# Loading the first strided values once instead of twice, in a fused attention and feed-forward kernel with a newly searched order

## The chip, the cores and the metric

The kernel runs on one core of one Trainium2 chip. The metric is device time in microseconds (us) for the whole program. The profiled execution is one run recorded by the hardware profiler; its span is the time from the core's first to its last instruction. Engines are named as in the profile: PE (matmul), PEld (its weight load), DVE, ACT, POOL and SP. SPq and ACTq are the sequencers of SP and ACT, from which transfers are issued.

## The reference

```python
def _attn_ref(q, k, v):                      # 8 batches, 8 heads, 576 positions, 64 channels
    scores = scale * np.matmul(q, k.transpose(0, 1, 3, 2))
    mask_local = (rel >= 0) & (rel < 32)                       # heads 0 to 3
    mask_strided = (rel >= 0) & (pos[None, :] % 32 == pos[:, None] % 32)   # heads 4 to 7
    scores = np.where(masks[None], scores, -1e9)
    attn = exp(scores - max) / (sum + 1e-9)
    return np.matmul(attn, v)

def _moe_ref(x, w_in, w_out, g_ln):          # x: 4608 tokens x 512
    h = x @ w_in                             # 512 x 1024
    sm = softmax(h)
    solu = h * sm
    ln = (solu - mean) / sqrt(var + 1e-6) * g_ln
    return ln @ w_out                        # 1024 x 512
```

The weights `w_in` and `w_out` arrive as 64-bit floating point numbers and are decoded on the chip.

## The kernel before

Each batch has two kinds of attention heads. Local heads look back over 32 positions, strided heads look at positions of the same residue modulo 32. The work of a batch is cut into five units: units 0 and 1 are the strided heads, units 2 to 4 the local ones. Unit numbers run on, so that unit 5 is the first of batch 1. A unit is a chain: `qk` (PE, lines 419 and 424), the row maximum, subtraction, sum and reciprocal (DVE, lines 430 to 438), the exponential (ACT, 432), the scaling (POOL, 441), an fp16 upper part (ACT, 446) and lower part (POOL 448 or DVE 450), a transpose of the probabilities through a DMA from `p` to `pt` (SP, 452), `pv` (PE, 473) into `x_ps`, and the fp16 upper and lower parts of the result, `xhi` (ACT, 489) and `xlo` (DVE, 490). The banks of `x_ps` that `pv` writes must have been read by the steps 489 and 490 of an earlier unit.

The feed-forward part takes 36 tiles of 128 tokens: `g1` (PE, 531 to 533, two halves of 12 matmuls) makes h from `xhi`, `xlo` and the two fp16 parts of `w_in`; DVE and ACT make the normalised rows (538 to 559), a DMA transposes them (570), and `g2` (PE, 574 to 576) multiplies with the two parts of `w_out`.

Weights come in four loads of 1 MB each for `w_in` and four for `w_out`, into the four rooms `room0`, `room1`, `eu0` and `eu1`. Each load is decoded by two ACT steps (599 and 600) and one DVE step (601). From the decoded `w_in` a power-of-two scale is made (`gram` on PE, line 295, then `pow2_scale`), and with it the two fp16 parts: the upper one on ACT (617), the lower one on DVE (619) or, for half of the weights, on PE (`rest`, 627 and 628) followed by an ACT copy (631). `w_out` has its own `gram` over the four decoded pieces, then `split_o` (653 and 654).

The values of batch 0's strided heads have a path of their own. They are loaded twice from HBM in the same layout into the buffer `vtwo`: `t0` into partitions 0 to 63 (from ACT's queue), `t1` into partitions 64 to 127 (from SP's queue). ACT then writes the fp16 upper part into all 128 partitions of `vd` (374, two instructions), and DVE the lower part into partitions 0 to 63 (375). The upper half of the partitions holds the upper part a second time, so that one pass of `pv` multiplies both parts of the probabilities. The scale for these values is made from a `gram` over all of `vtwo` and `vrl`. Later batches load 128 partitions once and spread the parts with copies inside SBUF (394).

All steps are recorded by `plan.add` with the data that they read and write, and are then emitted in the order of the table `ORDER`, which lists step numbers. Each engine's and each queue's own order follows from that table. A DMA for which an instruction waits stands in its issuer's order, and what stands behind it on that queue waits with it.

Of the kernel before, what the change touches and what calls it, by code (L numbers as in the profile page):

```python
# [13 lines left out]
ALU = mybir.AluOpType  # L14
# [3 lines left out]
B, H, S, D = 8, 8, 576, 64  # L18
# [3 lines left out]
P = 128  # L22
# [140 lines left out]
def attn_solu_kernel(ctx: ExitStack, tc: tile.TileContext, qloc, qstr, kloc, kstr, vloc, vstr, w_in, w_out, g, masks, out):  # L163
    nc = tc.nc
# [70 lines left out]
    def load(name, dst, src, w):  # L235
        e, q = ("act", nc.scalar) if name in ACTQ else ("sp", nc.sync)
        add(e, lambda: q.dma_start(dst, src), w=w)
# [515 lines left out]
```

## Time and profile before

| | |
|---|---|
| median of 3 runs | 506.12 us (504.93 to 506.67) |
| the profiled execution's own time | 507.28 us |
| its span, first to last instruction | 505.6 us |
| mean granted TensorE clock | 0.993 |
| PE busy | 473.5 us (94%) |
| DVE busy | 354.2 us (70%) |
| ACT busy | 294.0 us (58%) |
| POOL busy | 151.0 us (30%) |
| moved by DMA | 96.51 MB, mean 191 GB/s |
| read from HBM | 40.03 MB |

The rows of a timeline have the start in us, the length in us, the engine and line, the operation, the tile written and the tile read, the number of instructions, and in brackets the idle time of that engine just before them with what ended it. A row that covers several instructions starts with the first of them. The rows of transfers give the packets, bytes and rate of a stretch, or the issues of a kind with their size and the median time from issue to landing. Rows of stretches give, by engine, the busy time in us and the number of instructions, then the granted clock as a share of full speed, the busy share of the 16 DMA engines (which can exceed 1 where packets overlap) and GB/s. What lies between the end of the span and the execution's own time is 1.68 us.

### The profile page before, as it was taken

The page shows a single profiled execution, that of the slowest core. Times are in us where ns is not written, and L with a number is a line of the kernel's source. Part 1 is how long each engine was busy: PE and PEld are TensorE (multiplying, and loading weights), DVE is VectorE, ACT ScalarE, POOL GpSimd, SP SyncE. Part 2 cuts the span into 40 slices and gives each one's busy share as a digit, 9 for nine tenths or more (in the row PEclk, how much of TensorE's full clock was granted, in tenths as well). Part 3 has the DMA queues.
Part 4 walks back from the last instruction along what each step waited for, and adds up shares of the span by engine and source line. Part 5 has one row for each costly group of instructions (what it writes and reads, how often), then busy time and mean ns, then how long its engine had stood idle before and what let it go on. Part 6 is the DMA issues. An engine that isn't in the chain of part 4 may idle for free.

```text
span 505.6 us, 11821 instructions
## 1 busy us (share of the span) xinstructions
PE 473.5 (94%) x4858; PEld 246.7 (49%) x4858; DVE 354.2 (70%) x679; ACT 294.0 (58%) x414; POOL 151.0 (30%) x258
## 2 busy tenths in 40 slices
PE   2557999999999999999999999999999999999997
PEld 1444554455544554454544554455444555444443
DVE  2688798785873797589865986487954989645530
ACT  1698877853746557546646446653756466344631
POOL 3234153444150133305330153301430053312330
PEclk9998899999999999999999999999999999999999
DMA  8999999688977879966998999977977797652361
GB/s 256 397 327 269 306 196 176 184 200 186 191 152 205 215 174 171 274 158 150 172 250 179 201 206 217 232 181 163 219 164 203 165 191 129 116 106 62 88 141 64
DMA packets 168294, 96.51 MB, mean 191 GB/s; under 512 B 138032, under 2 KB 154800, under 8 KB 167728
## 3 DMA queue, kind: packets, MB, share of 16 engines
q1 hardware_dynamic: 162624, 84.77, 78.6%
q10 hardware_dynamic: 5616, 10.98, 6.5%
q8 instruction: 38, 0.62, 0.5%
q14 instruction: 16, 0.13, 0.1%
HBM read 40.03 MB, written 9.44 MB: 98 GB/s over the span
## 4 chain that ended last, share of the span: by engine, by line
PE 81%; DMA 9%; DVE 6%; issue 2%; ACT 1%; SPq 1%; POOL 0%; DVEq 0%; ACTq 0%
PE h_ps L531 12%; PE o_ps L574 11%; PE h_ps L532 11%; PE h_ps L533 11%; PE o_ps L575 11%; PE o_ps L576 11%; PE x_ps L473 5%; PE s_ps L424 5%; DMA vrl<-vloc 3%; DMA eu<-w_out 2%; PE s_ps L419 1%; DMA pt<-p 1%; DMA vtwo<-vstr 1%; DMA ct<-c 1%; PE s_ps L576 1%
## 5 line engine op out<-in xcount | busy, mean ns | idle before, releaser
L441 POOL TENSOR_TENSOR t<-t,m 128x576 f32<-128x576 f32 (+2 forms) x40 | 51.4, 1287 | 238.7 <-DVE m L438 180.0
L531 PE MATMUL h_ps<-w,xhi 128*128 128x512 f16 x280 | 106.6, 381 | 0.0
L532 PE MATMUL h_ps<-w,xhi 128*128 128x512 f16 x280 | 106.1, 379 | 0.0
L533 PE MATMUL h_ps<-w,xlo 128*128 128x512 f16 x280 | 106.1, 379 | 0.0
L574 PE MATMUL o_ps<-obuf,ct 128*128 128x512 f16 x272 | 103.4, 380 | 0.6 <-DMA ct<-c 0.5
L576 PE MATMUL o_ps<-obuf,ct 128*128 128x512 f16 x272 | 103.1, 379 | 0.0
L575 PE MATMUL o_ps<-obuf,ct 128*128 128x512 f16 x272 | 103.1, 379 | 0.0
L538 DVE TENSOR_REDUCE st<-h_ps 128x1 f32<-128x1024 f32 x35 | 42.7, 1220 | 39.5 <-PE h_ps L533 38.8
L549 ACT ACTIVATE eu<-h_ps,st,vsc 128x1024 f32<-128x1024 f32 x31 | 37.3, 1204 | 36.4 <-DVE st L539 31.1
L556 ACT ACTIVATE c<-eu,st 128x1024 f16<-128x1024 f32 x36 | 41.2, 1145 | 24.3 <-DVE st L555 22.8
L557 DVE SCALAR_TENSOR_TENSOR c<-eu,st,c 128x1024 f16<-128x1024 f32 x36 | 46.9, 1304 | 10.7 <-ACT c L556 10.6
L552 DVE SCALAR_TENSOR_TENSOR eu<-h_ps,st,eu 128x1024 f32<-128x1024 f32 x35 | 44.8, 1279 | 8.4 <-ACT eu L549 7.2
L424 PE MATMUL s_ps<-k,q 64*54 64x54 f32 (+1 forms) x1280 | 41.6, 272 | 5.4 <-DMA k<-kloc 3.7
L432 ACT ACTIVATE t<-t 128x576 f32<-128x576 f32 (+2 forms) x40 | 27.4, 686 | 31.9 <-DVE t L431 30.7
L533 PEld LDWEIGHTS <-xlo 128*128 128x128 f16 x288 | 28.2, 98 | 34.2 <-issue 0.3
L576 PEld LDWEIGHTS <-ct 128*128 128x128 f16 x288 | 28.2, 98 | 34.0
L531 PEld LDWEIGHTS <-xhi 128*128 128x128 f16 x288 | 28.2, 98 | 33.8 <-ACT w L631 0.7
L559 ACT ACTIVATE junk<-eu,st 128x1024 bf16<-128x1024 f32 x36 | 41.1, 1141 | 6.0 <-DVE st L555 3.7
L574 PEld LDWEIGHTS <-ct 128*128 128x128 f16 x288 | 28.1, 98 | 33.1 <-DMA ct<-c 1.0
L532 PEld LDWEIGHTS <-xhi 128*128 128x128 f16 x288 | 28.2, 98 | 31.4 <-issue 0.3
L575 PEld LDWEIGHTS <-ct 128*128 128x128 f16 x288 | 28.2, 98 | 30.5
L424 PEld LDWEIGHTS s_ps<-k,q 64*54 64x54 f32 (+1 forms) x1280 | 39.6, 199 | 6.2 <-issue 6.2
(148 smaller groups left out, 682.0 us busy)
## 6 DMA issues: line engine op xcount, KB each, us to landing
out<-ob ACTq DMA_DIRECT2D x36, 256.0 KB, 3.3
vtwo<-vstr SPq DMA_DIRECT2D x8, 768.0 KB, 6.8
vd<-vtwo SPq DMA_DIRECT2D x14, 384.0 KB, 6.9
vrl<-vloc SPq DMA_DIRECT2D x8, 640.0 KB, 6.2
k<-kstr SPq DMA_DIRECT2D x8, 594.0 KB, 5.2
q<-qloc SPq DMA_DIRECT2D x8, 576.0 KB, 5.8
k<-kloc SPq DMA_DIRECT2D x8, 576.0 KB, 6.6
q<-qstr SPq DMA_DIRECT2D x7, 594.0 KB, 5.6
```

The lines of the kernel that those rows point to most:

```text
L424: nc.tensor.matmul(s_ps[row : row + nq, pair, i * nk : (i + 1) * nk], q_raw[half][hs, q0 : q0 + (nq - 1) * nqb + 1 : nqb], k_raw[half][hs, ...
L441: add("pool", lambda: nc.gpsimd.tensor_tensor(tv, tv, sm.unsqueeze(2).broadcast_to([P, nx, nk]), op=ALU.mult), r=TM, w=[T])
L531: nc.tensor.matmul(hv[:, i], xhi[:, cc, tok], whi[:, cc, cols], start=(cc == 0), stop=False)
L532: nc.tensor.matmul(hv[:, i], xhi[:, cc, tok], wlo[:, cc, cols], start=False, stop=False)
L533: nc.tensor.matmul(hv[:, i], xlo[:, cc, tok], whi[:, cc, cols], start=False, stop=(cc == 3))
L538: add("dve", lambda: nc.vector.tensor_reduce(low, hv, axis=AX.XY, op=ALU.max, negate=True), r=HH, w=[(ST, "low")])
L552: add("dve", lambda: nc.vector.scalar_tensor_tensor(uv, hv, ia, ev, op0=ALU.mult, op1=ALU.mult, accum_out=us), r=[*HH, E, (ST, "ia")], w=[ ...
L556: add("act", lambda: nc.scalar.activation(c[:, 0], u, AF.Identity, bias=mean, scale=1.0), r=[U, (ST, "mean")], w=[(C, 0)])
L557: add("dve", lambda: nc.vector.scalar_tensor_tensor(c[:, 1], u, mean, c[:, 0], op0=ALU.add, op1=ALU.subtract), r=[U, (ST, "mean"), (C, 0)] ...
L574: nc.tensor.matmul(o, ct[:, cc, :], ohi[:, cc, :], start=(cc == 0), stop=False)
L575: nc.tensor.matmul(o, ct[:, cc, :], olo[:, cc, :], start=False, stop=False)
L576: nc.tensor.matmul(o, ct[:, 8 + cc, :], ohi[:, cc, :], start=False, stop=(cc == 7))
```

## The change

The load `t1` is dropped. The `gram` for the scale reads partitions 0 to 63 of `vtwo`, the two ACT steps write 64 partitions, and for each of them a DMA inside SBUF copies the upper part to partitions 64 to 127 of `vd`; `pv` of batch 0's strided units waits for these copies too. Two step numbers are added and one dropped, and the table `ORDER` is another one throughout.

```diff
 ORDER = [
-    11, 6, 10, 9, 14, 0, 13, 31, 15, 5, 18, 16, 2, 19, 7, 12, 4, 3, 69, 70, 71, 82, 72, 73, 58, 1, 74, 32, 83, 75, 8, 84, 17, 23, 76, 27, 126, 59, 143, 85,
+    11, 6, 10, 9, 30, 4, 13, 14, 18, 7, 17, 0, 22, 15, 2, 12, 3, 8, 1, 16, 5, 26, 70, 71, 72, 83, 73, 31, 74, 57, 262, 75, 32, 84, 76, 85, 33, 86, 58, 77, 19,
...
     def load_v(b, a):
         if b == 0 and a:
-            for i in range(2):
-                load(f"t{i}", vtwo[i * D : i * D + D].rearrange("p (y f) -> p y f", y=2), vstr[b].rearrange("(y p) f -> p y f", y=2),
-                     [("vr2", 1)] if i else [("vr", 1), ("v", 1, 0), ("v", 1, 1)])
+            load("t0", vtwo[0:D].rearrange("p (y f) -> p y f", y=2), vstr[b].rearrange("(y p) f -> p y f", y=2), [("vr", 1), ("v", 1, 0), ("v", 1, 1)])
             return
...
-            gram(vm[:, 0:1], [(vtwo, [("vr", 1), ("vr2", 1)]), (vr_sb[0], [("vr", 0)])], ("vm", 0, 0), (o_ps[:, 0:P], "o"), (junk[:, 0:P], "junk"))
+            gram(vm[:, 0:1], [(vtwo[0:D], [("vr", 1)]), (vr_sb[0], [("vr", 0)])], ("vm", 0, 0), (o_ps[:, 0:P], "o"), (junk[:, 0:P], "junk"))
...
-            R = [("vr", 1), ("vr2", 1), ("vsc", 0), ("v", 1, 0), ("v", 1, 1)]
+            R = [("vr", 1), ("vsc", 0), ("v", 1, 0), ("v", 1, 1)]
             for y in range(2):
-                hi, lo = vd_sb[:, 0, :, y], vd_sb[0:D, 1, :, y]
-                add("act", lambda y=y, hi=hi: nc.scalar.mul(hi, raw[:, :, y], sc[:, 1:2]), r=R, w=[("v2", 1, y)])
-                add("dve", ... stt(lo, raw[0:D, :, y], sc[0:D, 1:2], hi[0:D], ...), r=[*R, ("v2", 1, y)], w=[("v2", 1, 2 + y)])
+                hi, lo = vd_sb[0:D, 0, :, y], vd_sb[0:D, 1, :, y]
+                add("act", lambda y=y, hi=hi: nc.scalar.mul(hi, raw[0:D, :, y], sc[0:D, 1:2]), r=R, w=[("v2", 1, y)])
+                add("sp", lambda y=y, hi=hi: nc.sync.dma_start(vd_sb[D:P, 0, :, y], hi), r=[("v2", 1, y)], w=[("v2", 1, 4 + y)])
+                add("dve", ... stt(lo, raw[0:D, :, y], sc[0:D, 1:2], hi, ...), r=[*R, ("v2", 1, y)], w=[("v2", 1, 2 + y)])
...
-        VV = [("v2", half, i) for i in range(4 if half else 3)] + ...
+        VV = [("v2", half, i) for i in range(6 if half and b == 0 else 4 if half else 3)] + ...
```

The order of each queue moves with the table. In the rows below a name's last number is that of the buffer in the program, and the numbers before it are the kernel's own (`room1`, `eu0`). The first place is SP's queue from the start of the program. Before:

```order
L237 DMA k10_66<-kstr 128x1188
L237 DMA vtwo0_72<-vstr 64x2x1536
L237 DMA room1_68<-w_in 128x2048
L237 DMA vrl0_70<-vloc 128x1280
L237 DMA g0_124<-g 128x8
L237 DMA q00_63<-qloc 128x1152
L237 DMA eu0_103<-w_in 128x2048
L237 DMA k00_65<-kloc 128x1152
L237 DMA eu1_104<-w_in 128x2048
L237 DMA room0_67<-w_in 128x2048
```

After, the same stretch and on to the first transpose:

```order
L237 DMA room1_68<-w_in 128x2048
L237 DMA vrl0_70<-vloc 128x1280
L237 DMA eu0_103<-w_in 128x2048
L237 DMA g0_124<-g 128x8
L237 DMA eu1_104<-w_in 128x2048
L237 DMA q00_63<-qloc 128x1152
L237 DMA k00_65<-kloc 128x1152
L237 DMA room0_67<-w_in 128x2048
L237 DMA k10_66<-kstr 128x1188
L237 DMA vrl0_70<-vloc 128x1280
L373 DMA vd0_73<-vd0_73 64x6x256
L237 DMA vtwo0_72<-vstr 128x1536
```

The `t1` load (`64x2x1536`) is gone, the loads of `eu0` and `eu1` have moved ahead of `q00` and `k00`, batch 1's `k10` is loaded before its values, and the two copies `vd<-vd` stand around batch 1's `vtwo` load (the second right behind the last row shown).

The second place is SP's queue around the four loads of `w_out`. Before:

```order
L237 DMA room0_67<-w_out 128x2x1024
L452 DMA_TRANSPOSE pt1_100<-p1_97 128x10x128
L237 DMA room1_68<-w_out 128x2x1024
L394 DMA ve0_74<-vl0_71 64x2560
L452 DMA_TRANSPOSE pt0_99<-p2_98 128x12x128
L237 DMA eu1_104<-w_out 128x2x1024
L237 DMA eu0_103<-w_out 128x2x1024
```

After:

```order
L237 DMA room0_67<-w_out 128x2x1024
L451 DMA_TRANSPOSE pt1_100<-p1_97 128x10x128
L393 DMA ve0_74<-vl0_71 32x2x1024
L237 DMA eu0_103<-w_out 128x2x1024
L393 DMA ve0_74<-vl0_71 64x2560
L451 DMA_TRANSPOSE pt0_99<-p2_98 128x12x128
L237 DMA room1_68<-w_out 128x2x1024
L237 DMA eu1_104<-w_out 128x2x1024
```

Two of the four loads stand ahead of unit 2's transpose (`pt0<-p2`) in both; the other two follow it, as `eu1`, `eu0` before and as `room1`, `eu1` now.

The third place is ACT's queue where these loads are decoded and where the last pieces of `w_in`'s lower part are copied (`w16<-h_ps`), with unit 1's and unit 2's `xhi`. Before:

```order
L599 ACTIVATE obuf0_121<-room1_68 128x1024
L446 CAST p0_96<-t3_90 128x6x96
L489 CAST xhi0_101<-x_ps_129 128x2x18x15
L599 ACTIVATE obuf0_121<-room0_67 128x1024
L600 ACTIVATE room1_68<-room1_68,consts0_116 128x1024
L631 CAST w160_120<-h_ps_128 128x512
L489 CAST xhi0_101<-x_ps_129 128x2x192
L631 CAST w160_120<-h_ps_128 128x512
L600 ACTIVATE room0_67<-room0_67,consts0_116 128x1024
L631 CAST w160_120<-h_ps_128 128x512
L599 ACTIVATE obuf0_121<-eu0_103 128x1024
```

After:

```order
L598 ACTIVATE obuf0_121<-room0_67 128x1024
L488 CAST xhi0_101<-x_ps_129 128x2x18x15
L445 CAST p0_96<-t3_90 128x6x96
L630 CAST w160_120<-h_ps_128 128x512
L431 ACTIVATE t1_88<-t1_88 128x648
L599 ACTIVATE room0_67<-room0_67,consts0_116 128x1024
L598 ACTIVATE obuf0_121<-eu0_103 128x1024
L488 CAST xhi0_101<-x_ps_129 128x2x192
L630 CAST w160_120<-h_ps_128 128x512 x2
L599 ACTIVATE eu0_103<-eu0_103,consts0_116 128x1024
L630 CAST w160_120<-h_ps_128 128x512
L598 ACTIVATE obuf0_121<-room1_68 128x1024
```

Before, the first decode of `w_out` that ACT meets is that of the second load (`room1`), and unit 1's `xhi` stands behind it. Now it is that of the first load (`room0`), and the decodes follow in the order of the loads.

More of the change, by code (lines that the diff above doesn't have):

```diff
@@ L370, in v_split @@
             raw = vtwo.rearrange("p (y c f) -> p c y f", y=2, c=6)
-            R = [("vr", 1), ("vr2", 1), ("vsc", 0), ("v", 1, 0), ("v", 1, 1)]
+            R = [("vr", 1), ("vsc", 0), ("v", 1, 0), ("v", 1, 1)]
             for y in range(2):
-                hi, lo = vd_sb[:, 0, :, y], vd_sb[0:D, 1, :, y]
-                add("act", lambda y=y, hi=hi: nc.scalar.mul(hi, raw[:, :, y], sc[:, 1:2]), r=R, w=[("v2", 1, y)])
-                add("dve", lambda y=y, hi=hi, lo=lo: nc.vector.scalar_tensor_tensor(lo, raw[0:D, :, y], sc[0:D, 1:2], hi[0:D], op0=ALU.mult, op1=ALU.subtract), r=[*R, ("v2", 1, y)], w=[("v2", 1, 2 + y)])
+                hi, lo = vd_sb[0:D, 0, :, y], vd_sb[0:D, 1, :, y]
+                add("act", lambda y=y, hi=hi: nc.scalar.mul(hi, raw[0:D, :, y], sc[0:D, 1:2]), r=R, w=[("v2", 1, y)])
+                add("sp", lambda y=y, hi=hi: nc.sync.dma_start(vd_sb[D:P, 0, :, y], hi), r=[("v2", 1, y)], w=[("v2", 1, 4 + y)])
+                add("dve", lambda y=y, hi=hi, lo=lo: nc.vector.scalar_tensor_tensor(lo, raw[0:D, :, y], sc[0:D, 1:2], hi, op0=ALU.mult, op1=ALU.subtract), r=[*R, ("v2", 1, y)], w=[("v2", 1, 2 + y)])
             return
@@ L474, in pv @@
                                              start=(a == 0), stop=(a == len(passes) - 1))
-        VV = [("v2", half, i) for i in range(4 if half else 3)] + (["vz"] if half else []) + ([("v", 0, 0), ("v", 0, 1)] if half == 0 else [])
+        VV = [("v2", half, i) for i in range(6 if half and b == 0 else 4 if half else 3)] + (["vz"] if half else []) + ([("v", 0, 0), ("v", 0, 1)] if half == 0 else [])
         add("pe", pv, r=[PT, *VV], w=X)
```

94 rows, old and new, of the table ORDER are left out of this document.

## The prediction

> **What bounds the kernel now.** I read the span by stages first. After the stretch and its length, the columns are PE, PEld, DVE, ACT and POOL busy, the granted clock, the DMA share and GB/s.
>
> ```profile
> 0.00:50.00 50.00, 25.71 (x444) 18.99 (x444) 32.97 (x67) 31.96 (x36) 16.49 (x37) 0.97 1.03 311
> 50.00:70.00 20.00, 18.21 (x184) 9.80 (x184) 16.57 (x34) 15.23 (x21) 6.94 (x5) 0.91 1.16 264
> 70.00:480.00 410.00, 407.69 (x4131) 208.23 (x4131) 300.11 (x572) 240.62 (x350) 123.10 (x207) 1.00 0.85 178
> 480.00:505.60 25.60, 21.88 (x102) 9.72 (x100) 4.54 (x8) 6.21 (x9) 4.43 (x11) 0.99 0.43 105
> ```
>
> From 70 to 480 us PE idles 410.00 − 407.69 = 2.3 us: PE is the bound there. The edited loads lie in the first 50 us, where PE idles 24.3 us and the DMA engines are full (share 1.03). The change can win only by letting PE's dense stretch begin earlier. So I read PE's timeline from its last long gap on.
>
> ```profile
> 46.79 1.12 PE L627 MATMUL h_ps<-c,wdiag 128*128 128x512 f32 x2
> 47.76 0.38 PE L628 MATMUL h_ps<-w,minus 128*128 128x512 f16 x1
> 50.61 0.28 PE L473 MATMUL x_ps<-pt,ve 96*64 96x64 f16 x6 [2.48 <-DVE xlo L490]
> 51.55 2.08 PE L627 MATMUL h_ps<-c,wdiag 128*128 128x512 f32 x2
> 53.85 0.61 PE L531 MATMUL h_ps<-w,xhi 128*128 128x512 f16 x1
> 59.04 0.38 PE L533 MATMUL h_ps<-w,xlo 128*128 128x512 f16 x1
> 63.83 0.63 PE L295 MATMUL o_ps<-obuf 128*128 128x128 bf16 x8 [0.57 <-DVE obuf L601]
> 64.30 0.38 PE L531 MATMUL h_ps<-w,xhi 128*128 128x512 f16 x1
> 67.35 0.16 PE L315 MATMUL o_ps<-o_sc,ones 128*128 128x1 bf16 x1 [0.30 <-DVE o_sc L645]
> ```
>
> Unit 2's `pv` starts at 50.61 after 2.48 us idle, tile 0's `g1` runs from 53.85 to about 59.3, tile 1's starts at 64.30. Two waits hold this stretch back. Both lead to ACT and the decode of `w_out`.
>
> ```profile
> 47.60 1.14 ACT L599 ACTIVATE obuf<-room 128x1024 f32<-128x1024 f32 x1 [1.30 <-DMA room<-w_out]
> 49.21 0.60 ACT L489 CAST xhi<-x_ps 128x540 f16<-128x540 f32 x1
> 52.31 0.47 ACT L489 CAST xhi<-x_ps 128x384 f16<-128x384 f32 x1
> 52.69 0.58 ACT L631 CAST w<-h_ps 128x512 f16<-128x512 f32 x1
> 56.83 1.14 ACT L599 ACTIVATE obuf<-eu 128x1024 f32<-128x1024 f32 x1 [1.96 <-DMA eu<-w_out]
> ```
> ```profile
> 49.84 0.72 DVE L490 TENSOR_TENSOR xlo<-x_ps,xhi 128x540 f16<-128x540 f32 x1 [1.11 <-ACT xhi L489]
> 60.88 1.22 DVE L538 TENSOR_REDUCE st<-h_ps 128x1 f32<-128x1024 f32 x1
> 62.56 1.21 DVE L601 SCALAR_TENSOR_TENSOR obuf<-obuf,eu 128x1024 int32<-128x1024 int32 x1
> ```
>
> ACT waits until 47.60 for the second `w_out` load, unit 1's `xhi` (49.21) and `xlo` (49.84) follow late, and PE's gap ends with that `xlo`. The fourth load reaches ACT at 56.83; its last decode step on DVE ends at 63.77, and PE's last `gram` matmuls wait for it.
>
> **The change part by part.** *Loads and copies.* The price of the DMA's time comes from three stretches (packets, MB, rate) and the issue row of the later batches' like copies.
>
> ```profile
> DMA packets 425, 2.37 MB, mean 279 GB/s; under 512 B 45, under 2 KB 45, under 8 KB 364
> DMA packets 728, 4.39 MB, mean 419 GB/s; under 512 B 83, under 2 KB 89, under 8 KB 343
> DMA packets 703, 0.35 MB, mean 176 GB/s; under 512 B 16, under 2 KB 703, under 8 KB 703
> vd<-vtwo SPq DMA_DIRECT2D x2, 192.0 KB, 5.2
> ```
>
> The first is 5 to 13.5 us, with `t0` and `t1` in it; the second is 18 to 28.5, of big loads; the third is 62 to 64, only 512-byte copies into `vd`. `t1` is 64 x 3072 x 4 B = 0.786 MB: 2.8 us at 279 GB/s. If it cost no more than any other load it is 1.9 us at 419; if the two half-partition loads caused the whole shortfall of that stretch (2.37 MB would take 5.65 us at 419, so 2.85 us) it is 1.9 + 2.85 = 4.7. The two copies move 0.393 MB: 2.2 us at 176 GB/s, 0.9 at 419, and at most 2.6 if each held the engines for half of the 5.2 us that its kind takes to land. I take the middle values, since these rows hold the same shapes: −2.8 + 2.2 = −0.6 us of DMA time, with ends −3.8 and +0.7.
>
> The Trainium skill, page "SBUF — State Buffer", section "Can I just issue two DMAs to hit both halves?", states that two transfers to partitions 0 and 64 serialise, with 6% gained; its "Door 1" section gives 64 partitions about half the ports. An estimate from its 196 GB/s for 64 partitions would make `t1` 4.0 us, the copies 2.0, and the sum −2.0 instead of −0.6. The trace agrees in direction (279 against 419 GB/s), and the high end above covers it.
>
> *Other work of this part.* ACT's two steps on 64 partitions cost what they did on 128:
>
> ```profile
> 23.36 3.53 DVE L375 SCALAR_TENSOR_TENSOR vd<-vtwo,vsc,vd 64x1536 f16<-64x1536 f32 x2
> 46.94 1.79 DVE L380 SCALAR_TENSOR_TENSOR vtwo<-vtwo,vsc 128x1536 f16<-128x1536 f32 x1
> 21.34 3.03 ACT L374 ACTIVATE vd<-vtwo,vsc 128x1536 f16<-128x1536 f32 x2
> 23.51 0.33 SPq L237 DMA_DIRECT2D vrl<-vloc  x1
> 26.92 0.34 SPq L237 DMA_DIRECT2D vtwo<-vstr  x1
> 36.15 0.94 PE L473 MATMUL x_ps<-pt,vd 118*64 118x54 f16 x48
> ```
>
> The shorter `gram` also stays as long. The copies wait for ACT, whose steps end at 24.4; SP before it waits anyway until 23.51 and 26.92 to issue batch 1's values, so no queue is held longer. Issued by 27.3, at 5.2 us the copies land near 32.5, ahead of unit 0's `pv` at 36.15: 3.6 us of cover, so I cost them at nothing on PE. If they landed over 3.6 us late, PE would still have its other idle time there.
>
> *The queue orders.* Unit 2's transpose and the four loads:
>
> ```profile
> 32.55 0.39 SPq L237 DMA_DIRECT2D room<-w_out  x1
> 39.04 0.57 SPq L237 DMA_DIRECT2D room<-w_out  x1
> 40.38 4.87 SPq L452 DMA_TRANSPOSE pt<-p  x1
> pt<-p SPq DMA_TRANSPOSE x1, 9.8
> 45.97 10.84 DMA eu<-w_out
> ```
>
> The fourth row is the landing time of that transpose: 40.38 + 9.8 = 50.2. In the new order ACT's first decode uses the first load, issued 6.5 us before the second, so 1.30 us of waiting disappear and unit 1's `xlo` no longer ends PE's gap. What is late next is the transpose, at 50.2 − 0.6 = 49.6. Unit 2's `pv` moves from 50.61 to 49.6: −1.0 us.
>
> *Up to the first `g1`.* Between `pv` and `g1` stand 2 + 1 `rest` matmuls. They take 53.85 − 51.55 = 2.30 us here and 48.14 − 46.79 = 1.35 at 46.79. The clock rows say why.
>
> ```profile
> 46.00:48.00 2.00, 2.00 (x38) 1.13 (x34) 1.97 (x4) 0.70 (x2) 0.83 (x1) 1.00 1.72 106
> 51.00:52.00 1.00, 1.00 (x25) 0.94 (x21) 0.90 (x3) 1.00 (x2) 0.00 (x0) 0.50 0.98 393
> ```
>
> The granted clock is 0.50 after the 2.48 us gap and 1.00 before it. With PE's work still ending near 48.1 the gap shrinks to 1.5 us or less, and I assume that the clock stays up. That gives 0.95 us, of which ACT takes 0.25 back: `pv` ends at 50.5, then `xhi` (0.47) and two copies (0.58 each) bring `g1` to 52.2 rather than 51.9. So `g1` starts 1.7 us earlier; with the clock halved, 1.0.
>
> The Trainium skill, page "TensorE: Matmul & The Clock Gate", section "What's actually happening", lets the clock halve after an idle window of about 3.4 us. Here 2.48 us was enough, so the measurement decides; by the page the shorter gap would keep the full clock.
>
> *From tile 0 to tile 1.* With 0.2 us more gained where tile 0's first matmuls ran at half clock, it ends at 59.3 − 1.9 = 57.4. The last load lands at 45.97 + 10.84 = 56.8, minus 0.6 = 56.2; its two ACT steps (about 1.1 each) end at 58.4. On DVE the row reduction after tile 0 (1.22), small steps (0.46, the space before 62.56) and the last decode (1.21) end near 60.3. The DVE steps for the scale follow, and their PE step now stands ahead of tile 1's `g1`. Here that step runs at 67.35, 3.6 us after the decode's end at 63.77, with steps of other units and tiles in between; in the new order fewer stand there, and I take 2.0, which is an estimate (at 3.6 tile 1 would start at 64.0). So tile 1 starts at 62.4 instead of 64.30 (−1.9). The wait of 0.30 at 67.35 is gone too. Sum: **−2.2 us**.
>
> *The rest.* The profiled execution took 507.28 us, 1.16 above the median of 506.12. 507.28 − 2.2 = 505.1; put on the median, **503.9 us**. In the middle the order is new throughout, but PE's waits from 68 to 480 are small, so little can be won there. The two longest (total, times, longest):
>
> ```profile
> PE x_ps L473 <- DMA pt<-p: 0.8, 1, 0.8
> PE o_ps L574 <- DMA ct<-c: 0.5, 1, 0.5
> ```
>
> I count it as 0, with ±2.3 us, its whole idle time, as bounds. The tail after 480 has nothing of the change in it.
>
> **The rivals.** *The gain is eaten.* The copies take 2.6 us and the dropped load saves only 1.9, so the transpose lands at 50.9, 0.3 us after the start of today's `pv`; the gap stays long enough for the clock to halve, and tile 1 waits as today. That gives −0.1 to −0.5, about 505.8. For it: the DMA engines are full until 66 us and a DVE chain of 3.6 us instead of 2.0 would by itself hold tile 1 until 64.0. Against it: ACT's waits of 1.30 and 1.96 go by the order alone.
>
> *A larger relief.* The half-partition load cost 4.0 us, so the transpose and the last load land about 2 us earlier rather than 0.6. The start of tile 1 then hangs on DVE alone, and tile 0 ends 0.9 us sooner: −3.1, 503.0.
>
> *Slower: a transpose comes late in the new order.* In the old order one unit, 24, had 21.7 us of PE's work between its `qk` and its `pv` (added up over the order with the rows' durations) and waited 0.8 us for `pt`, the first row above. In the new order unit 33 has 19.7, before 33.8. If its chain takes unit 24's 22.5 us, PE idles 2.8 us, and a gap of that length halves the clock as at 50.61, where it cost 0.95 + 0.2 us and can cost twice that in a stretch of nothing but PE's work: 4.5 in all, 506.12 − 2.2 + 4.5 = 508.4. It decides when the stall costs over 3.7 us. Against it: other units ran with 15.6 (unit 14) and 18.2 (unit 29) and never waited.
>
> **How the numbers follow.** Some 0.3%, 1.5 us, is about what a measurement of this kernel can tell from no change, so under 504.6 is faster and over 507.6 slower. Forecast 0.43, its own range 502.6 to 505.0, five sixths of it faster; gain eaten 0.27; larger relief 0.14; late transpose 0.16, of which 0.02 stays under 507.6. Faster: 0.36 + 0.14 = 0.50. Same: 0.07 + 0.27 + 0.02 = 0.36. Slower: 0.14. The range runs from 501.6 (larger relief, and half of the middle's idle time won) to 507.0 (gain eaten, and a small new wait), and leaves out most of the late transpose.
>
> **What would show it.** Right: ACT's first decode of `w_out` starts before 46 without a wait; PE's gap before unit 2's `pv` under 1.6 us, granted clock 1.00 at 51; first `g1` near 52.2, tile 1's near 62.4; the copies into `vd` landed before 33. Wrong: a gap ended by the transpose after 50.5, a clock of 0.50 again, or any wait of PE over 1 us between 70 and 480.

## The result: 1.1% slower

The changed kernel takes 511.41 us (median of 4 runs, 511.25 to 512.29) against 506.39 us for the kernel before on the same measurement; the ratio is 1.0108, with a 95% interval from 1.0084 to 1.0132. Forecast was 503.9. The profiled execution has a span of 509.5 us (before: 505.6). Its stages, in the columns of the prediction (PE, PEld, DVE, ACT, POOL busy, clock, DMA share, GB/s; the last stretch runs past the end of the span):

```profile
0.00:50.00 50.00, 24.67 (x444) 19.32 (x445) 34.44 (x69) 33.65 (x37) 20.14 (x37) 0.97 1.03 305
50.00:70.00 20.00, 18.13 (x208) 10.26 (x208) 17.31 (x36) 14.94 (x21) 6.59 (x6) 0.91 1.17 256
70.00:480.00 410.00, 404.73 (x4100) 206.30 (x4093) 297.70 (x568) 237.51 (x345) 123.76 (x209) 1.00 0.85 178
480.00:520.00 40.00, 25.87 (x120) 11.56 (x118) 6.17 (x10) 8.36 (x13) 2.85 (x8) 0.99 0.34 73
```

PE's total busy time is the same in both (473.4 and 473.5 us), so the 3.9 us of span come out as idle time: 1.1 us more in the first 70 us (27.2 against 26.1), 3.0 us more from 70 to 480 (5.27 against 2.31), and nothing in the tail. Matmuls at half clock take longer and count as busy, so these figures alone don't say where the delay arises. Where PE's dense stretch begins, the new kernel reads so:

```profile
9.78 1.50 PE L423 MATMUL s_ps<-k,q 64*54 64x54 f32 x48 [3.02 <-DMA q<-qstr]
50.11 0.37 PE L472 MATMUL x_ps<-pt,ve 96*64 96x64 f16 x6 [2.31 <-DVE vsc L361]
51.21 2.08 PE L626 MATMUL h_ps<-c,wdiag 128*128 128x512 f32 x2
53.47 0.38 PE L530 MATMUL h_ps<-w,xhi 128*128 128x512 f16 x1
61.98 0.63 PE L295 MATMUL o_ps<-obuf 128*128 128x128 bf16 x8 [0.99 <-DVE obuf L600]
64.28 0.16 PE L315 MATMUL o_ps<-o_sc,ones 128*128 128x1 bf16 x1 [0.76 <-DVE o_sc L644]
64.31 0.38 PE L530 MATMUL h_ps<-w,xhi 128*128 128x512 f16 x1
```

The row of 50.11 names a DVE step (`vsc`, which ends at 50.06) as what ended the gap, but `pv` reads nothing of that step; the transpose that it needs lands at 50.1. Tile 0's `g1` starts 0.4 us earlier than before (53.47 against 53.85) and tile 1's at the same time (64.31 against 64.30), with the step for the scale of `w_out` already done (before: at 67.35). The `pv` behind tile 1 starts at 69.62 against 70.06. So at 70 us the kernel is 0.4 us ahead, and what it loses, it loses behind that. There come PE's waits between 70 and 480 us, among them one that did not exist before, for unit 34 (the last unit of batch 6):

```profile
414.70 0.28 PE L472 MATMUL x_ps<-pt,ve 96*64 96x64 f16 x6 [1.91 <-DMA pt<-p]
416.00:418.00 2.00, 2.00 (x27) 1.01 (x20) 1.05 (x2) 2.00 (x3) 1.45 (x5) 0.50 0.91 192
```

The granted clock is 0.50 behind that wait. On SP's queue, before and after (start, length of the issue):

```profile
401.33 1.43 SPq L452 DMA_TRANSPOSE pt<-p  x1
403.06 5.90 SPq L394 DMA_DIRECT2D vd<-vtwo  x4
```
```profile
402.04 3.96 SPq L393 DMA_DIRECT2D vd<-vtwo  x3
406.14 4.08 SPq L451 DMA_TRANSPOSE pt<-p  x1
```

Before, the transpose goes out at 401.33, ahead of batch 7's copies into `vd`, and lands in 5.2 us. Now it goes out at 406.14 behind three of these copies and lands in 8.5 us.

Times of one kernel scatter by 1 to 2 us in either direction, so the experiments below are read by their ratios to the kernel before, taken on the same chip in the same session.

### The profile page after: what moved, and what is told of

It is laid out like the page before. It is cut to its first block, busy times and chain, and to the rows that moved or that the text cites. A ratio compares the mean times of both kernels' runs of the same rounds, so it can differ in the third digit from the quotient of the medians.

```text
span 509.5 us, 11822 instructions
## 1 busy us (share of the span) xinstructions
PE 473.4 (93%) x4858; PEld 247.4 (49%) x4858; DVE 355.6 (70%) x679; ACT 294.5 (58%) x414; POOL 153.3 (30%) x258
```

## The experiments

| run | loads | order | median us | ratio to before, 95% interval |
|---|---|---|---|---|
| changed kernel | new | new | 511.41 | 1.0108 (1.0084 to 1.0132) |
| e7, the same again | new | new | 511.93 | 1.0115 (1.0089 to 1.0142) |
| e1 | old | new | 509.99 | 1.0073 (1.0049 to 1.0098) |
| e2 | new | old | 506.99 | 1.0019 (1.0005 to 1.0033) |
| e3 | new | new start, old rest | 509.23 | 1.0072 (1.0054 to 1.0091) |
| e9 | new | old start, new rest | 511.21 | 1.0104 (1.0068 to 1.0140) |
| e4 | new | new, copies behind unit 34's transpose | 509.84 | 1.0084 (1.0068 to 1.0100) |
| e13 | new | new, unit 34 early | 509.50 | 1.0070 (1.0051 to 1.0088) |
| e14 | old | new, unit 34 early | 507.40 | 1.0030 (1.0011 to 1.0049) |
| e15 | new | e13, unit 1's transpose first | 508.33 | 1.0044 (1.0023 to 1.0065) |
| e10 | new | e9, unit 34 early | 509.08 | 1.0049 (1.0028 to 1.0069) |
| e11 | old | old, unit 34 late | 510.64 | 1.0073 (1.0048 to 1.0098) |
| e5 | new, copies by POOL | old | 508.23 | 1.0039 (1.0023 to 1.0056) |
| e6 | new, `q10` behind `k10` | old | 507.59 | 1.0031 (1.0012 to 1.0050) |
| e8 | e5 and e6 | old | 506.40 | 1.0002 (0.9989 to 1.0016) |
| e16 | old, `q10` behind `k10` | old | 505.55 | 0.9985 (0.9972 to 0.9998) |
| e17 | new, copies from ACT's queue | e13 | 509.12 | 1.0057 (1.0035 to 1.0080) |
| e18 | e17 and `q10` behind `k10` | e15 | 508.34 | 1.0046 (1.0030 to 1.0061) |

0.001 of the ratio is 0.5 us. In the listings of experiments with a rewritten table `ORDER` the line numbers are 12 to 14 lower.

### Loads or order

The change has two halves, which the steps' numbers let one take apart.

**e1**: the old loads in the new order.

```diff
 SP's queue, from the start (the rest of the order is the new one)
 k<-kstr
+vtwo<-vstr      (t1, partitions 64 to 127)
 room<-w_in
```

> The kernel before (t1 loaded, no copies) with the changed kernel's order; t1 keeps its old place, second on SP's queue. Theory O (the new order costs the time, in the middle of the program): about 511, with a wait of PE for unit 34's transpose near 413 and the clock at half speed behind it. Theory L (the dropped load and the copies cost it): about 506.

**e2**: the new loads in the old order.

```diff
 SP's queue near 24 us, in the order of before
 vrl<-vloc
+vd<-vd          (copy)
 ve<-vl x2
 vtwo<-vstr
+vd<-vd          (copy)
 pt<-p           (unit 0)
```

> The changed kernel with the order of before; the two copies stand behind batch 1's two value loads on SP's queue. Theory O: 505.5 to 506.5, no new wait of PE after 70 us. Theory L: about 510, with the first qk over 1 us late and new waits behind it.

Measured: e1 +0.73%, with a wait of 1.91 us for unit 34's transpose, which ends at 413.12; e2 +0.19%. Most of the loss is the order's, as theory O has it, but e2 refutes its second half: the load change alone is no gain and costs 0.3 to 1.7 us.

**e3** and **e9** cut the order at tile 1's first matmuls.

```diff
 ORDER (e3)
-new order throughout
+new order up to tile 1's first g1 step, then the old order of all steps left
 ORDER (e9)
-new order throughout
+old order up to tile 1's first g1 step, then the new order of all steps left
```

> The changed kernel in its own order up to the first matmuls of tile 1, and in the order of before from there on. Theory O: tile 1 starts at 64.3 as in the changed kernel, the middle has no wait over 1 us, 505.0 to 506.0. Theory L: 510 to 511, since all of the load change is in it.

> The new loads, the old order up to the first matmuls of tile 1, and the new order from there on: the other half of e3. If start and rest of the order add up (new start 2.2 us by e3 against e2, new rest 2.2 to 2.7 by the changed kernel against e3), 507.0 + 2.5 = 509.5, with the wait for unit 34's transpose near 413. If the loss comes from the two new parts together, 507 to 508.

Measured: e3 +0.72%, over 3 us more than expected; e9 +1.04%. Both have the new loads; above e2's 0.19%, e3's half of the new order costs 0.53% and e9's 0.85%, where the whole costs 0.92%. The two don't add up. e3's trace has a wait of 1.60 us for a transpose right behind the cut, at 71.9, but e4 and e7, which have no cut there, have one of 1.47 us at the same place. So these two only say that the start is not free either. I leave the size of each half at that.

**e7** and **e12** are the two kernels once more.

```diff
 (no edit)
```

> The changed kernel once more, on the chip of the others: 510.5 to 511.5, with PE's wait of 1.5 us or more for unit 34's transpose near 413. If the wait is not there in this execution, the time of the profiled execution is 2 to 3.6 us lower.

> The kernel before, unchanged, for a second trace: the first qk near 8.5 and the start of tile 0's g1 within 1.5 us of 53.85, the four small waits of the middle again between 0 and 1.7 us.

Measured: 511.93 and 507.2 us. In e7 the wait for unit 34 is there again (2.36 us), but this time the granted clock stays at 1.00 behind it, so the half clock is no fixed part of its price. In the second trace of before the wait is not there; the first `qk` starts at 8.68, `g1` at 53.40, and the middle has three waits of 1.8, 0.3 and 0.2 us.

### Unit 34's transpose

**e4** moves only SP's queue.

```diff
 SP's queue near 402 us
-vd<-vtwo x3
 pt<-p           (unit 34)
+vd<-vtwo x3
```

> The changed kernel with one move on SP's queue: three of batch 7's copies into vd stand behind unit 34's transpose instead of ahead of it. Theory O, if the DMA traffic of these copies is the cause: the transpose lands in 6 us instead of 8.5, PE's wait of 1.9 us and the half clock behind it go (1.9 + 1.7), 507.8. If the late DVE and POOL steps of unit 34 are the cause instead, over half of the wait stays and the time is 510 to 511. Theory L: 511.

Measured: +0.84% instead of +1.08 to 1.15%, and the wait for unit 34 is gone; the wait of 0.60 us that is left near there is for unit 35's transpose. Up to that point e4 runs 2.7 us later than the changed kernel, so its times must be read from the unit's `qk` on. Unit 34's transpose goes out 10.3 us after its `qk`, at 408.83, as late as in the changed kernel: `p` isn't ready sooner. But it lands in 4.7 us instead of 8.5, and `pv` starts at 415.41 without a wait. So it is the three copies ahead of the transpose that turn a late `p` into a wait.

**e13** (from the changed kernel) and **e10** (from e9) move the chain that makes `p` too.

```diff
 DVE, POOL and ACT near 400 us
 row sum of unit 34
+reciprocal, scaling and fp16 upper part of unit 34
 maximum and subtraction of unit 35
 ...
-reciprocal, scaling and fp16 upper part of unit 34
 SP's queue
-vd<-vtwo x3
 pt<-p           (unit 34)
+vd<-vtwo x3
```

> The changed kernel with unit 34's chain brought forward as in e10 (its DVE, POOL and ACT steps ahead of units 35 and 36, its transpose ahead of the three copies into vd). Theory O: the wait of 1.9 to 2.4 us near 413 and the half clock behind it go, 511.7 - 3.6 = 508.1. If it falls by under 2 us, other parts of the new order have taken the wait over.

> As e9, and unit 34's chain is brought forward: its DVE, POOL and ACT steps ahead of units 35 and 36, and its transpose ahead of the three copies into vd. Theory O (this one chain is the new rest's loss): no wait near 413 and the clock stays at full speed, 507.0 to 507.5. If the new rest loses its time in the small waits for ct and scales instead: 508.5 to 509.5.

Measured: e13 +0.70%, e10 +0.49% against +1.04% for e9. The wait is gone in both, and the clock stays at 1.00; e10's stretch:

```profile
405.51 1.43 SPq L438 DMA_TRANSPOSE pt<-p  x1
412.00:414.00 2.00, 2.00 (x11) 0.93 (x10) 1.99 (x3) 1.53 (x3) 1.02 (x1) 1.00 1.16 182
414.00:416.00 2.00, 2.00 (x67) 1.51 (x65) 1.97 (x6) 0.86 (x1) 0.26 (x1) 1.00 1.07 179
```

So unit 34 is worth 2.1 us of the changed kernel's 5.6 (0.0112 against 0.0070), not the expected 3.6. From e9 to e10 it is 2.8.

**e11** does the reverse to the kernel before.

```diff
 SP's queue near 401 us, in the kernel before
-pt<-p           (unit 34)
 vd<-vtwo x3
+pt<-p           (unit 34)
 vd<-vtwo
```

> The kernel before with one move: unit 34's transpose is issued behind three of batch 7's copies into vd, as in the changed kernel. Theory O: it is issued near 406 instead of 401.3 and lands 8.5 us later near 414.5, PE waits some 2.5 us for it and runs at half clock for 3 us behind it: 506.4 + 2.5 + 1.5 = 510.4. If PE's idle time there is made up elsewhere: under 508.

Measured: 510.64 us, +0.73%. This one move makes two thirds of the changed kernel's loss, with its marks: issue at 407.46, PE's wait, half clock.

```profile
407.46 4.07 SPq L439 DMA_TRANSPOSE pt<-p  x1
415.38 0.37 PE L460 MATMUL x_ps<-pt,ve 96*64 96x64 f16 x6 [2.46 <-DMA pt<-p]
416.00:418.00 2.00, 2.00 (x25) 1.00 (x20) 0.35 (x1) 1.42 (x3) 0.00 (x0) 0.50 1.08 232
```

### The new loads

**e14** is e13 with the old loads.

```diff
 SP's queue
 k<-kstr
+vtwo<-vstr      (t1)
 ...
-vd<-vd x2
```

> As e13 with the old loads (t1 loaded, no copies). If the load change costs its 0.9 us here too: 507.2, near the kernel before. If it costs nothing in the new order: as e13, 508.1.

Measured: +0.30%, 2.0 us under e13; between e1 and the changed kernel, the other pair that differs in the loads alone, it is 1.9 us. In e14's trace the new order's start is near what the prediction worked out, 51.7 for the first `g1` (52.2 forecast):

```profile
49.40 0.28 PE L460 MATMUL x_ps<-pt,ve 96*64 96x64 f16 x6 [1.82 <-DMA pt<-p]
51.71 0.39 PE L518 MATMUL h_ps<-w,xhi 128*128 128x512 f16 x1 [0.28 <-ACT w L618]
```

In e13, the same order with the new loads, these rows read

```profile
53.13 0.28 PE L459 MATMUL x_ps<-pt,ve 96*64 96x64 f16 x6 [3.42 <-DMA pt<-p]
55.70 0.63 PE L517 MATMUL h_ps<-w,xhi 128*128 128x512 f16 x1
```

One pair of traces could be scatter, since e13 is the changed kernel's own program up to 400 us. But all traces of these two starts agree in direction: in the new order tile 0's `g1` starts at 51.71 and 52.98 with the old loads (e14, e1) and at 53.47 to 55.70 with the new ones (the changed kernel, e3, e4, e7, e13); in the old order it starts at 53.40 to 53.85 (before, e11, e12) and at 54.90 to 55.89 (e2, e9, e10). The changed kernel's own trace is the earliest of its kind, which is why it shows so little of this delay.

What the loads do between is seen on SP's queue. Unit 0's transpose stands behind the two copies; its issue in the changed kernel, in e13, in e14 and in the kernel before:

```profile
27.99 5.11 SPq L451 DMA_TRANSPOSE pt<-p  x1
```
```profile
27.62 6.00 SPq L438 DMA_TRANSPOSE pt<-p  x1
```
```profile
28.47 2.07 SPq L439 DMA_TRANSPOSE pt<-p  x1
```
```profile
27.36 3.27 SPq L452 DMA_TRANSPOSE pt<-p  x1
```

With the copies ahead of it the issue holds SP for 4.7 to 6.0 us (all ten traces of kernels that issue them from SP), with the old loads for 2.1 to 4.2 (six traces). What stands behind it on the queue goes out later, from e14 to e13 the first `w_out` load by 1.9 us (33.20 to 35.12) and unit 2's transpose by 3.1 (38.60 to 41.70). In e2, where the order is the old one, batch 1's values come later too, and the second `w_out` load holds ACT and with it `xlo` and `pv` of unit 2, the very chain that the new order was to shorten:

```profile
34.88 1.48 ACT L341 ACTIVATE junk<-vtwo 128x1536 bf16<-128x1536 f32 x1 [2.10 <-DMA vtwo<-vstr]
49.77 1.12 ACT L585 ACTIVATE obuf<-room 128x1024 f32<-128x1024 f32 x1 [2.31 <-DMA room<-w_out]
52.77 0.28 PE L459 MATMUL x_ps<-pt,ve 96*64 96x64 f16 x6 [3.33 <-DVE xlo L476]
```

(before: 47.60 for the second row and 50.61 for the third.) Not all of a late start reaches the end. In e2's trace tile 0's `g1` starts 2.0 us later than before (55.89 against 53.85), but PE then idles only 0.47 us from 70 to 480 instead of 2.31, and the span is 505.1 us against 505.6.

**e5** takes the copies off the DMA engines.

```diff
-add("sp", lambda y=y, hi=hi: nc.sync.dma_start(vd_sb[D:P, 0, :, y], hi), ...)
+add("pool", lambda y=y, hi=hi: nc.gpsimd.tensor_copy(vd_sb[D:P, 0, :, y], hi), ...)
```

> As e2 (the new loads in the old order), but POOL copies the upper parts to partitions 64 to 127 instead of the two DMAs; POOL was idle there from 19.4 to 28.5 us. Theory C (the two copies hold up batch 1's values and unit 0's transpose, which are queued behind them): ACT's wait for batch 1's vtwo falls from 2.1 to about 1 us, the second w_out load is issued near 39 instead of 40.1, unit 2's pv starts near 50.6 instead of 52.8; 505.3 to 506.1. Theory Q (the first qk is 1.1 us late because the 1 MB load now competes with q10): no change from e2, 507.0.

Measured: +0.39%, no better than e2. The issue of unit 0's transpose does fall to 1.54 us, and tile 0's `g1` starts at 53.89 instead of e2's 55.89. But POOL's copies take 4.66 us, and DVE's lower parts beside them 5.95 instead of e2's 3.54, so batch 1's values can only be loaded from 29.10 on instead of 27.05.

```profile
23.12 5.95 DVE L361 SCALAR_TENSOR_TENSOR vd<-vtwo,vsc,vd 64x1536 f16<-64x1536 f32 x2
22.80 4.66 POOL L360 COPY vd<-vd 64x1536 f16<-64x1536 f16 x2 [4.29 <-ACT vd L359]
```

Its earlier start did not reach the end: its trace has waits of 1.7 us for `ct` and 0.4 for `vd` near 200 us, e2's has neither.

**e6** and **e8** are about the first load.

```diff
-ACTQ = {"mask", "q10", "t0"}
+ACTQ = {"mask", "t0"}
```

> As e2 with its DMA copies, but q10 is issued from SP directly behind k10 and ahead of the 1 MB load of w_in. Both theories: the first qk starts before 8.5 instead of 9.6. Theory Q: that 1 us reaches the start of tile 0's g1, 505.5 to 506.2. Theory C: it is lost again by 35 us, where PE waits for batch 1's values; 507.0.

> Both edits of e5 and e6 together in the old order. Theory C: as e5, 505.3 to 506.1. Theory Q: as e6. If both count: 504.5 to 505.3, below the kernel before.

Measured: e6 +0.31%, no better than e2, with the first `qk` at 9.01 instead of 9.57. e8 +0.02%: with both edits the load change costs nothing that can be measured, and gains nothing. As parts of one sum they make no sense (e5 and e6 are each no better than e2, together they are). The traces show where an earlier start goes: PE idles 2.52, 2.15 and 1.57 us from 70 to 480 in e5, e6 and e8, most of it in waits for `ct` and `vd` near 200 us. Why these waits differ so is not explained.

**e17** and **e18** issue the copies from ACT's queue.

```diff
-add("sp", lambda y=y, hi=hi: nc.sync.dma_start(vd_sb[D:P, 0, :, y], hi), ...)
+add("act", lambda y=y, hi=hi: nc.scalar.dma_start(vd_sb[D:P, 0, :, y], hi), ...)
 # e18 also
-ACTQ = {"mask", "q10", "t0"}
+ACTQ = {"mask", "t0"}
 # and, on SP's queue
-room<-w_out, pt<-p (unit 1)
+pt<-p (unit 1), room<-w_out
```

> As e13 (unit 34 early, new loads, new order), but the two copies are issued from ACT's queue right behind the ACT steps that write the upper part. If SP's queue is what they hold up: unit 0's transpose is issued in 2 to 3 us instead of 5 to 6, unit 1's and unit 2's pv wait under 2 us, tile 0's g1 starts near 53, 507.4. If it is their traffic: the issue still takes 5 us, 509.5.

> As e17, with unit 1's transpose ahead of the first w_out load (e15) and q10 on SP's queue directly behind k10 (e16). If the gains add up: 1.2 + 0.5 below e17, 505.7. If the start's gains replace each other: as e17.

Measured: +0.57% and +0.46%, against +0.70% for e13 and +0.44% for e15, whose order e18 shares. Their intervals overlap, so no gain is shown. SP's issue of unit 0's transpose falls to 3.35 and 4.27 us, which points to the copies' place on SP's queue as a part of what makes it long, and not as the whole. ACT pays: it stands idle for 0.72 and 0.68 us around the two issues (1.24 us together), right ahead of the decodes of `w_in`. How much of the copies' cost is the queue and how much their traffic is not settled by this.

### The start's order

**e15** moves one transpose ahead of a 1 MB load.

```diff
 SP's queue near 35 us, in e13
-room<-w_out
 pt<-p           (unit 1)
+room<-w_out
```

> As e13, with unit 1's transpose issued ahead of the first w_out load instead of behind it. If the 1 MB load is what makes that transpose late (PE waited 1.0 to 2.5 us for it): the wait is under 0.7, tile 0's g1 starts some 1 us earlier, and the time is 0.5 to 1 us below e13. If the start is held by the full DMA engines whatever the order: the same as e13.

Measured: +0.44%, 1.3 us under e13. PE's wait for unit 1's transpose falls from 2.29 us to none (0.20, for DVE), tile 0's `g1` starts at 53.48 instead of 55.70. The intervals of e13 and e15 overlap, and 53.48 is within what traces of the changed kernel's start show without this edit (53.47 to 55.70), so the gain is likely and not certain.

**e16** is e6's edit on the kernel before.

> The kernel before (old loads, old order) with q10 issued from SP directly behind k10. First qk near 7.5 instead of 8.5 to 8.7. If an earlier start reaches the end: 505.3 or below. If it is given back later (by the waits for ct and vd near 200 us): within 0.5 of 506.2.

Measured: 0.9985 (0.9972 to 0.9998), the one kernel below the kernel before, by 0.1 to 1.4 us. Its first `qk` starts at 9.10, later than before's 8.48 and not near 7.5: `q10` lands in 7.7 us from SP as in 7.1 from ACT. So the reason is not the one for which I tried it. The trace shows the values of `t0` landing in 10.5 us instead of 12.7, and tile 0's `g1` at 52.91 instead of 53.85 (53.40 in e12).

## Why the prediction was wrong

**Right: the chain of ACT.** ACT decodes the first `w_out` load at 43.45 without a wait and casts unit 1's `xhi` at 44.51 (before: 49.21). PE's gap then ends with the transpose of unit 2: issued at 40.61, it takes 9.5 us, 50.1. Forecast was 49.6.

**Wrong: the net of the DMA time, −0.6 us.** It has the wrong sign on this path. On SP's queue batch 0's `k10` still goes first (at 0.79 us in both kernels), and right behind it now goes, instead of `t1`, a 1 MB load of `w_in`. That load gains: it lands in 7.6 us instead of 14.0. `q10`, for which PE waits, takes 8.4 us instead of 7.1: the first `qk` starts at 8.5 to 8.9 in the five traces with the old loads and the old place of `q10`, and at 9.5 to 10.1 in the eleven with the new loads and that place. That the one load slows the other is argued from their places; putting `q10` ahead of it brings the new loads to 8.9 to 9.0 (e6, e8, e18). And the copies are not paid in bytes.

**Wrong: "no queue is held longer", the copies at nothing.** This is the step of the load change that failed. I looked at whether the copies land ahead of the `pv` that reads them (they do, 7.2 us after their issue instead of 5.2, near 34.5 instead of before 33, with `pv` at 37.47), and not at what they delay. How much of that is the queue and how much the copies' traffic stays open (e17). The larger relief by half-partition loads did not come either: e2 and e14 against e13 show a loss of 1 to 2 us.

**Undecided: the clock.** The gap before unit 2's `pv` was 2.31 us, not 1.5 (PE's work ended at 47.80 and not near 48.1, and the transpose landed 0.5 us later than forecast), and the clock fell to 0.50 as before. In e7, with a gap of 2.33 us at the same place of the same program, it stayed at 1.00:

```profile
50.00:70.00 20.00, 16.51 (x184) 9.30 (x185) 16.91 (x35) 15.45 (x22) 6.52 (x6) 1.00 1.20 266
```

So a gap near 2.3 us halves the clock in one execution and not in the next; e7's time (511.92 for that execution) was no better for it.

**Wrong: from tile 0 to tile 1.** The DVE steps from the end of the last decode to the scale took 61.93 to 64.23, 2.3 us, close to the 2.0 of the estimate. But the last decode ended at 61.93 and not at 60.3, and tile 1 started at 64.31 and not at 62.4. In the changed kernel tile 0's `g1` ended late, near 58.9 instead of 57.4. The late start isn't all of it, though. e14 started tile 0's `g1` at 51.71, earlier than forecast, with the clock at 1.00 from 50 to 70 us, and its tile 1 was no earlier:

```profile
64.55 0.16 PE L302 MATMUL o_ps<-o_sc,ones 128*128 128x1 bf16 x1 [0.65 <-DVE o_sc L632]
64.57 0.38 PE L518 MATMUL h_ps<-w,xhi 128*128 128x512 f16 x1
```

There DVE was busy with another decode step until 59.31 (2.31 us for it instead of 1.22), then came the row reduction, and the last decode ended at 62.28. So what the start had won was lost again on DVE; the outcome is that of the rival of the eaten gain, though not by its cause. Of the forecast −2.2 us, −0.4 was left at 70 us in the changed kernel.

**Wrong: the middle at 0 ± 2.3.** This is the largest term. The rival of the late transpose had the mechanism (a transpose behind its due time, the half clock behind the wait), with the wrong unit and too small a chance; its price of 4.5 us was measured at 2.1 (e13), 2.8 (e10 against e9) and 3.7 (e11). I compared PE's work between `qk` and `pv`, unit by unit, saw that units with little of it had not waited, and stopped. Unit 34 has little of it, too (the wait begins 16.9 us after its `qk`, 395.9 to 412.8; before, 19.4 us lay between). But what decides is whether the unit's chain fits in there. Before, the transpose was issued 8.7 us after the `qk` and landed in 5.2: 13.9 of 19.4 us. Now it takes 10.3 us to the issue and 8.5 to the landing, 18.8 of 16.9, and PE waits for the 1.9 that are missing. On DVE, unit 34's row sum, the reciprocal's first step and the lower part of `p` now stand like this:

```profile
399.12 0.74 DVE L432 TENSOR_REDUCE m<-t 128x6 f32<-128x576 f32 x1
402.88 0.17 DVE L436 TENSOR_SCALAR m<-m 128x6 f32<-128x6 f32 x1
405.37 0.75 DVE L449 TENSOR_TENSOR p<-t,p 128x576 f16<-128x576 f32 x1
```

Between the first two stand steps of unit 35 and of a tile, between the last two steps of units 35 and 36. The longer landing goes with the three copies that were put ahead (4.7 us without them in e4). Both stand in the order, for anyone who looks at the unit's rows on DVE and SP.

In sum, the changed kernel's 5.6 us (the mean of its two ratios) come apart into 2.1 for unit 34 (to e13), 2.0 for the new loads (to e14), and 1.5 for the rest of the new order. By the intervals the last is known to 1 us and the other two to some 1.3, and the shares depend on the order in which they are taken (unit 34 alone costs 3.7 us in the old order, the loads alone 0.9). The cause of the last part stays open; the runs show pieces only: a transpose of unit 1 behind a 1 MB load (e15), and waits for `ct` near 210 and 294 us that come and go between executions, up to 1.62 us in e14, which idles 1.45 us more than before from 70 to 480. The chance of 0.14 for slower rested on the order alone. That the loads themselves cost time was in none of the cases; the nearest, the eaten gain, ended at no change.

## What to carry to other kernels

A transfer that lands in time may still be dear: ask what it delays, behind it on its queue and beside it on the DMA engines, and who waits for that. When a table of order is replaced, compare for every unit the whole chain between two steps of the bound engine (its steps on each engine, and what its DMA stands behind) with the work that must cover it; one transfer put behind three copies cost 2.4 to 5.0 us in 506 (e11). Time won ahead of a dense stretch isn't won yet: look for the next wait in it.

## What the hardware showed unexpectedly

POOL copying 64 x 1536 fp16 twice (4.66 us) slowed DVE's two steps beside it from 3.54 to 5.95 us. The Trainium skill, page "SBUF — State Buffer", section "Who interferes with whom", states that a DVE instruction with two SBUF inputs contends with a GpSimd instruction that reads SBUF; DVE's step has two, and the 2.4 us agree with it. And a DMA's issue is no fixed price: that of unit 0's transpose held SP for 1.54 us in e5, 2.1 to 4.2 with the old loads, and 4.7 to 6.0 behind the two copies.
